# One POOL product of the retention's keys becomes four ACT activations, from the second block on

## The chip, the cores and the metric

The kernel runs on one core of one Trainium2 chip. The metric is the device time of one execution in microseconds (us). Five engines of the core work side by side, each through its own instruction stream: PE (matmul; PEld is its weight load), DVE, ACT, POOL, and SP, which only issues DMAs here.

## The reference

Three layers follow one another on 2304 tokens (4 batches of 576), all in float32:

```python
def _attn_ref(q, k, v):                 # (4, 8, 576, 64)
    scores = scale * np.matmul(q, k.transpose(0, 1, 3, 2))
    gamma = 1.0 - 2.0 ** (-5.0 - np.arange(H))
    Dmat = np.where(rel >= 0, gamma[:, None, None] ** rel, 0.0)
    return np.matmul(scores * Dmat, v)
...
def _moe_ref(x, domain_probs, w1, w2):  # 4 experts, all used by every token
    out += p[:, e:e + 1] * (np.maximum(x @ w1[e], 0.0) @ w2[e])
...
def _moe2_ref(...):                     # 8 experts, one per token by argmax of a gate
    out[mask] = gate_w[mask, None] * eom[mask, e, None] * (np.maximum(x[mask] @ w1[e], 0) @ w2[e])
```

The first layer is retention: attention without softmax, with a decay `gamma[h] ** distance` for each of the 8 heads.

## The kernel before

**Retention in chunks.** Each batch has 9 chunks of 64 positions, so there are 36 steps `s`. Within a chunk, masked scores are multiplied with v. Across chunks a state of k times v is carried and decays by `gamma ** 64` a chunk. For that state each key is first multiplied by `gamma ** (64 - i)`, where `i` is its position in the chunk: this product is `ks`. In the key's layout (partition = two halves of 64 positions, four blocks of 64 columns for four heads each) the factor is one number per partition and block: the table `ktab`, 128 x 4. `ks` is 128 x 256 float32 and isn't needed in the last chunk of a batch.

**A step.** `at_step(s)` issues, in this order, the products of q with the carried state (`at_past`, L273), the scores of the next chunk (`at_scores`, L250, then the mask on DVE, L255), the products of scores with v (`at_b`, L282), the state's new part from `ks[s+1]` (`at_state`, L297), the sum of the state on DVE (`at_sum`, L314), the output `xf` on DVE (L331), its float16 high half on ACT (L333) and its low half on POOL (L335), and last `at_split(s + 2)`, which makes `ks[s+2]` (L229). `ks` has three buffers. Its input is the second half of the tile `vkr`, which SP loads four steps ahead (L221), as soon as the buffer of four steps before is free.

**Blocks.** Four steps make one block of 256 tokens. When a block is complete, `x_mix` forms four differences in place in `xf` on POOL (L343), and, two steps later in the source, `x_keep` splits them into two float16 halves: high halves by two activations (L352, ACT), low halves on POOL (L353). The blocks are stored to DRAM and read back later.

**What runs around it.** The first expert's layers run on the finished blocks between the steps: `l1_first` (L515, with relu and split on ACT L501 and DVE L502) for blocks 0 to 4, and `l2` (L665, L673). After each such unit a hook runs one retention step. Meanwhile the expert weights are combined on POOL (L446) and split into float16 halves on ACT (L200, L201) and DVE (L202). From about 155 us on there is no retention work left, and the rest of the experts, the routing and the second expert layer follow.

**Order.** The kernel's source gives a program order; the compiler's scheduler then sets one fixed order for each engine from dependences, from that program order and from its own estimate of when an input is ready. Each engine works through its list in that order. `tc.issue_after` in the code is a hint to this scheduler, and `pace` holds the instructions that it hangs on.

Of the kernel before, what the change touches and what calls it, by code (L numbers as in the profile page):

```python
# [13 lines left out]
ACTF = mybir.ActivationFunctionType  # L14
ALU = mybir.AluOpType
# [4 lines left out]
B, H, S, D = 4, 8, 576, 64  # L20
# [18 lines left out]
NS = BT // C  # L39
# [91 lines left out]
def kernel(  # L131
# [19 lines left out]
    pe, act, dve, pool, sp = nc.tensor, nc.scalar, nc.vector, nc.gpsimd, nc.sync  # L151
# [17 lines left out]
    def cst(name, *dims):  # L169
        t, at = (ka, of_a) if name in of_a else (kb, of_b)  # L170
        o, n = at[name]
        a = t[:, o:o + n]
        if len(dims) == 2:
            return a.rearrange("p (a b) -> p a b", a=dims[0])
        return a
# [37 lines left out]
    raws, pm, st, uos, pace = {}, {}, {}, {}, {}  # L213
# [10 lines left out]
    def at_split(s):  # L224

        ks = None
        if s % NC < NC - 1:
            ks = at_1.tile([128, 4, D], F32, name="ks")
            pool.tensor_tensor(  # L229
                out=ks, in0=raws[s][1][:, 4:8], in1=cst("ktab", 4, 1).to_broadcast([128, 4, D]), op=ALU.mult  # L230
            )
        raws[s] += (ks,)

    def after(b, a):
# [123 lines left out]
    def at_step(s):  # L358

        at_open(s)  # L360
        at_past(s)
        if s + 1 < NSTEP:
            at_scores(s + 1)
        at_b(s)
        if s + 1 < NSTEP:
            at_state(s + 1, s)
            at_sum(s + 1, s)
        at_out(s)
        if s + 2 < NSTEP:
            at_split(s + 2)  # L370
# [710 lines left out]
    def opening(s):  # L1081
# [3 lines left out]


    at_split(0)
    at_scores(0)
    at_open(-1)
    at_state(0, -1)  # L1090
    at_sum(0, -1)
    at_split(1)
    opening(0)
    opening(1)
# [40 lines left out]
        out=p_sb, in0=p_sb, scalar=SO1, in1=ps_inv.to_broadcast([128, NT, E1]), op0=ALU.mult, op1=ALU.mult  # L1135
# [294 lines left out]
```

## Time and profile before

| | |
|---|---|
| median of 3 runs | 1009.02 us (1006.04 to 1009.07) |
| profiled execution | 1009.17 us, its span 1007.3 us |
| busy in the span | PE 963.7, DVE 578.2, ACT 527.0, POOL 411.8 us |
| retention's steps | from the start to about 160 us |

The span runs from the first to the last instruction of the profiled execution; 1.9 us of its time lie outside. Busy time of an engine is the time in which it executes; a wait is idle time that a profile row puts down to whatever released it. Lines such as L297 are those of the kernel's source, which is printed above.

### The profile page before, as it was taken

What the parts mean: (1) busy time and instruction counts of PE and PEld (TensorE: products, weight loads), DVE (VectorE), ACT (ScalarE), POOL (GpSimd) and SP (SyncE); (2) the same over time, 40 slices, a digit from 0 to 9 for tenths busy, and PEclk for the clock granted to TensorE, in tenths of its full rate; (3) what the DMA queues carried; (4) which work ended last, traced back from release to release, by engine and by line L of the source; (5) the groups of instructions that cost most, each with busy time, mean ns of one, the idle gap of its engine ahead of it and who ended that gap; (6) DMA issues with size and microseconds to landing.
All of it is one profiled execution on the core that took longest, in us unless ns stands there. A gap on an engine that the chain in (4) does not pass through costs nothing. (4 is left out here: it accounts for less than half of the span.)

```text
span 1007.3 us, 31905 instructions
## 1 busy us (share of the span) xinstructions
PE 963.7 (96%) x13507; PEld 827.4 (82%) x13507; DVE 578.2 (57%) x1297; ACT 527.0 (52%) x1001; POOL 411.8 (41%) x432
## 2 busy tenths in 40 slices
PE   5889999999999999999999999999999999999995
PEld 5566677889999999999999999999988677777773
DVE  5645462377767777776777676788888211211210
ACT  3235352487767777767778676666643112212221
POOL 3798874344436324525433453243223212112211
PEclk9999999999999999999999999999999999999998
DMA  9869875247455777556768725778946615554691
GB/s 336 281 225 320 265 238 195 71 153 249 137 177 174 246 272 233 189 183 177 228 205 275 271 85 152 215 201 206 233 133 233 232 43 218 199 231 137 254 395 48
DMA packets 95939, 209.48 MB, mean 208 GB/s; under 512 B 21486, under 2 KB 42222, under 8 KB 93488
## 3 DMA queue, kind: packets, MB, share of 16 engines
q1 hardware_dynamic: 82784, 159.20, 47.7%
q0 software_dynamic: 13008, 48.20, 15.0%
q8 instruction: 108, 1.77, 0.7%
q14 instruction: 39, 0.32, 0.1%
HBM read 197.88 MB, written 52.99 MB: 249 GB/s over the span
## 5 line engine op out<-in xcount | busy, mean ns | idle before, releaser
L628 PEld LDWEIGHTS <-op 128*128 128x128 f16 x2604 | 245.4, 98 | 27.0 <-issue 1.9
L562 POOL TENSOR_TENSOR op<-sm,op 128x512 f16<-128x512 f32 x124 | 142.3, 1157 | 279.8 <-ACT op L561 279.5
L543 PEld LDWEIGHTS <-wm_a 128*128 128x128 f16 x3264 | 192.8, 98 | 7.5 <-issue 3.6
L543 PE MATMUL ph<-xc,wm_a 128*128 128x128 f16 x2112 | 132.2, 219 | 2.9 <-DVE pq L603 2.9
L561 ACT ACTIVATE op<-sm 128x512 f16<-128x512 f32 x124 | 77.4, 633 | 81.5 <-DVE sm L566 81.5
L1048 DVE SCALAR_TENSOR_TENSOR h_s<-p_h,h_s 128x512 f16<-128x512 f32 x40 | 27.6, 691 | 159.1 <-ACT h_s L1047 159.1
L1055 PE MATMUL p_y<-wm_a,h_s 128*128 128x512 f16 x480 | 107.2, 379 | 0.5 <-DVE h_s L1048 0.5
L446 POOL TENSOR_TENSOR wr<-wr 128x512 f32<-128x512 f32 x64 | 81.2, 1274 | 43.1 <-ACT pz L200 39.4
L202 DVE TENSOR_TENSOR s<-pz,s 128x512 f16<-128x512 f32 x128 | 85.4, 683 | 22.4 <-ACT s L201 22.4
L628 PE MATMUL pv<-wm_a,op 128*128 128x256 f16 x792 | 97.6, 273 | 0.0
L628 PE MATMUL px<-wm_a,op 128*128 128x256 f16 x744 | 91.4, 272 | 1.1 <-DVE acc L636 1.1
L1055 PEld LDWEIGHTS <-h_s 128*128 128x128 f16 x480 | 46.7, 98 | 52.4 <-DVE h_s L1048 0.7
L200 ACT ACTIVATE pz<-sr 128x512 f32<-128x512 f32 x128 | 75.4, 603 | 17.0 <-DVE rk L784 10.6
L543 PEld LDWEIGHTS <-wm_b 128*128 128x128 f16 x1296 | 76.9, 98 | 2.2 <-issue 0.9
L1058 POOL DMA_INDIRECT out_dram<-y_s,sidxm x17 | 17.2, 1013 | 146.1 <-ACT y_s L1057 129.0
L201 ACT ACTIVATE s<-pz 128x512 f16<-128x512 f32 x128 | 73.7, 598 | 0.6
L1047 ACT ACTIVATE h_s<-p_h 128x512 f16<-128x512 f32 x40 | 23.9, 597 | 79.1 <-PE p_h L1038 73.2
L636 DVE SCALAR_TENSOR_TENSOR acc<-px,p_sb,acc 128x256 f32<-128x256 f32 x124 | 59.0, 476 | 8.3 <-PE px L628 8.2
L1038 PEld LDWEIGHTS <-wm_b 128*128 128x128 f16 x1056 | 60.0, 98 | 2.8 <-issue 0.6
L1057 ACT ACTIVATE y_s<-p_y,x_g 128x512 f32<-128x512 f32 x20 | 13.7, 687 | 92.5 <-PE p_y L1055 78.9
L1038 PE MATMUL p_h<-x_s,wm_b 128*128 128x128 f16 x1056 | 61.6, 219 | 0.3 <-issue 0.2
L200 ACT ACTIVATE pz<-wr 128x512 f32<-128x512 f32 x100 | 59.6, 607 | 2.3 <-DVE wm_a L202 1.2
(203 smaller groups left out, 1729.7 us busy)
## 6 DMA issues: line engine op xcount, KB each, us to landing
wm_a<-w2d SPq DMA_DIRECT2D x20, 2048.0 KB, 9.0
wr<-in_w_dram SPq DMA_DIRECT2D x40, 512.0 KB, 6.4
wm_b<-w1d SPq DMA_DIRECT2D x10, 2048.0 KB
wm_a<-w1d SPq DMA_DIRECT2D x10, 2048.0 KB
sr<-in_w1s_dram SPq DMA_DIRECT2D x64, 256.0 KB, 4.5
w1d<-s SPq DMA_DIRECT2D x64, 256.0 KB, 6.2
sr<-in_w2s_dram SPq DMA_DIRECT2D x64, 256.0 KB, 4.9
w2d<-s SPq DMA_DIRECT2D x64, 256.0 KB, 4.3
```

What stands on the lines that cost most here:

```text
L200: act.activation(out=z, in_=raw, func=ACTF.Copy, scale=scale)
L201: act.activation(out=hi, in_=z, func=ACTF.Copy)
L202: dve.tensor_tensor(out=lo, in0=z, in1=hi, op=ALU.subtract)
L446: pace["pool"] = pool.tensor_tensor(out=quarter(e, n, k, to), in0=quarter(e, n, k, x), in1=quarter(e, n, k, y), op=op)
L543: pe.matmul(bank[:, i], lhsT=w[:, k, u, 128 * i:128 * i + 128], rhs=x[:, v, d, k], start=(first and i == 0 and n == 0), stop=(n == 5), ski ...
L561: act.activation(out=hi, in_=s, func=ACTF.Copy)
L562: pool.tensor_tensor(out=lo, in0=s, in1=hi, op=ALU.subtract)
L628: pe.matmul(out, lhsT=o[a][:, v, k], rhs=w[c][:, k, u], start=(first and n == 0), stop=(n == 11), skip_group_check=True,)
L636: dve.scalar_tensor_tensor(out=a, in0=src, scalar=p_sb[:, b * TB + i, e:e + 1], in1=a, op0=ALU.mult, op1=ALU.add)
L1038: pe.matmul(ph[:, j], lhsT=w[k][:, x, f * 128:(f + 1) * 128], rhs=xs[:, y, k], start=(n == 0), stop=(n == 3 * KD - 1),)
L1048: dve.scalar_tensor_tensor(out=lo, in0=ph, scalar=0.0, in1=hi, op0=ALU.max, op1=ALU.subtract)
L1055: pe.matmul(po, lhsT=h[:, a, k], rhs=w[k][:, b], start=(n == 0), stop=(n == 3 * KF - 1))
```

## The change

For the first six chunks (`s < NS + 2`, with NS = 4) the keys are multiplied on POOL as before. For all later ones the same product is made by four activations on ACT, one for each block of 64 columns, each with its own scale per partition. Nothing else is edited; `ks` has the same shape, type, buffers and reader.

```diff
         if s % NC < NC - 1:
             ks = at_1.tile([128, 4, D], F32, name="ks")
-            pool.tensor_tensor(
-                out=ks, in0=raws[s][1][:, 4:8], in1=cst("ktab", 4, 1).to_broadcast([128, 4, D]), op=ALU.mult
-            )
+            k = raws[s][1][:, 4:8]
+            if s < NS + 2:
+                pool.tensor_tensor(out=ks, in0=k, in1=cst("ktab", 4, 1).to_broadcast([128, 4, D]), op=ALU.mult)
+            else:
+                for i in range(4):
+                    act.activation(out=ks[:, i], in_=k[:, i], func=ACTF.Copy, scale=cst("ktab")[:, i:i + 1])
```

## Rows read from the trace of the kernel before

**Rows 1.** The page's first part: span and busy time.
```profile
span 1007.3 us, 31905 instructions
...
PE 963.7 (96%) x13507; PEld 827.4 (82%) x13507; DVE 578.2 (57%) x1297; ACT 527.0 (52%) x1001; POOL 411.8 (41%) x432
```

**Rows 2.** Busy time by stretch: length, PE, PEld, DVE, ACT, POOL, clock, DMA.
```profile
25.00:150.00 125.00, 112.62 (x2316) 79.39 (x2314) 70.05 (x203) 51.62 (x105) 103.16 (x130) 0.97 0.80 265
```

**Rows 3.** Waits of PE from 0 to 400 us: total, times, longest.
```profile
PE uo L297 <- POOL ks L229: 6.4, 4, 2.6
```

**Rows 4.** Timeline of PE: start, us, instruction, idle before it and releaser.
```profile
52.53 0.46 PE L297 MATMUL uo<-vkr,ks 64*64 64x64 f32 x16 [1.71 <-POOL ks L229]
...
59.16 0.52 PE L297 MATMUL uo<-vkr,ks 64*64 64x64 f32 x16 [2.61 <-POOL ks L229]
...
63.23 0.46 PE L297 MATMUL uo<-vkr,ks 64*64 64x64 f32 x16
...
126.18 0.46 PE L297 MATMUL uo<-vkr,ks 64*64 64x64 f32 x16 [1.79 <-POOL ks L229]
```

**Rows 5.** Two stretches after those waits, columns as in rows 2.
```profile
59.00:63.00 4.00, 3.84 (x73) 2.85 (x73) 1.52 (x6) 2.90 (x7) 4.00 (x6) 0.57 0.47 187
127.00:131.00 4.00, 4.00 (x30) 2.77 (x32) 0.90 (x4) 0.54 (x2) 3.94 (x7) 0.59 0.82 293
```

**Rows 6.** Timeline of POOL around the waits.
```profile
51.86 0.61 POOL L229 TENSOR_TENSOR ks<-vkr,ka 128x256 f32<-128x256 f32 x1
...
55.68 0.68 POOL L335 TENSOR_TENSOR xc<-xf,xc 128x256 f16<-128x256 f32 x1
...
58.42 0.68 POOL L229 TENSOR_TENSOR ks<-vkr,ka 128x256 f32<-128x256 f32 x1
58.99 0.79 POOL L343 TENSOR_TENSOR xf<-xf 128x256 f32<-128x256 f32 x1
...
125.41 0.71 POOL L229 TENSOR_TENSOR ks<-vkr,ka 128x256 f32<-128x256 f32 x1
```

**Rows 7.** Timeline of SP: the load of chunk 11's `vkr`.
```profile
46.11 0.35 SPq L221 DMA_DIRECT2D vkr<-in_vk_dram  x1
```

**Rows 8.** DMA issues from 40 to 70 us: count, KB each, median us to landing.
```profile
qkr<-in_qk_dram SPq DMA_DIRECT2D x8, 320.0 KB, 5.2
```

**Rows 9.** Line 229 from 25 to 150 us: duration ns min/median/max.
```profile
L229 POOL TENSOR_TENSOR ks<-vkr,ka x26: 610/671/1056, 27.0 to 144.0; 128x256 f32<-128x256 f32 x26
```

**Rows 10.** Groups by form from 0 to 330 us: busy, mean ns, idle before.
```profile
L673 ACT ACTIVATE acc<-po,p_sb 128x512 f32<-128x512 f32 x10 | 6.8, 682 | 7.4 <-PE po L665 7.4
...
L501 ACT ACTIVATE ht<-ph 128x512 f16<-128x512 f32 x16 | 9.5, 595 | 14.3 <-PE ph L515 14.3
...
L191 ACT ACTIVATE wg_sb<-wgr 128x64 f16<-128x64 f32 x1 | 0.2, 248 | 0.0
```

**Rows 11.** Timeline of ACT.
```profile
39.17 1.14 ACT L352 ACTIVATE xc<-xf 128x512 f16<-128x512 f32 x2
...
58.57 0.63 ACT L352 ACTIVATE xc<-xf 128x512 f16<-128x512 f32 x1 [11.51 <-POOL xf L343]
59.11 0.40 ACT L333 ACTIVATE xo<-xf 128x256 f16<-128x256 f32 x1
...
76.93 0.60 ACT L501 ACTIVATE ht<-ph 128x512 f16<-128x512 f32 x1 [0.62 <-PE ph L515]
...
99.89 0.42 ACT L333 ACTIVATE xo<-xf 128x256 f16<-128x256 f32 x1 [1.85 <-DVE xf L331]
...
120.87 0.63 ACT L352 ACTIVATE xm<-xf 128x512 f16<-128x512 f32 x1 [8.06 <-POOL xf L343]
```

**Rows 12.** Timeline of DVE: step 8's `xf`.
```profile
48.12 0.42 DVE L331 TENSOR_TENSOR xf<-uo,ka 128x256 f32<-128x256 f32 x1
```

**Rows 13.** Timeline of PE: a wait for DVE.
```profile
81.02 0.46 PE L273 MATMUL uo<-qkr,sn 64*64 64x64 f32 x16 [0.33 <-DVE xf L331]
```

**Rows 14.** Waits of PE from 150 to 790 us, the longest.
```profile
PE ph L543 <- DVE pq L603: 3.6, 5, 0.8
```

## The prediction

> **What bounds the kernel now.** I read the page first. PE is busy for 963.7 of 1007.3 us [rows 1], so the end moves only if PE's idle time, or the work of a slow-clocked PE, moves. The change touches the retention's stage alone, so I read that stage by itself: from 25 to 150 us PE is busy for 112.62 of 125 us, POOL for 103.16 (83%) and ACT for 51.62 (41%) [rows 2]. POOL is the loaded engine here, and the edit takes work from it and gives it to a half idle one. Whether that is worth anything is read from PE's list of waits: PE waited 6.4 us in four places for POOL's `ks` [rows 3], and the timeline shows the three that matter, 1.71 us in step 9, 2.61 us in step 10 and 1.79 us in step 27 [rows 4] (the fourth is the remaining 0.3).
>
> After the second and third of them the granted clock falls: its mean is 0.57 over 59 to 63 us and 0.59 over 127 to 131 us [rows 5], that is, most of each stretch at 1.2 instead of 2.4 GHz. With PE busy nearly throughout, 4 x (1 - 0.57) = 1.7 us and 4 x (1 - 0.59) = 1.6 us of work were lost. The first wait, of 1.71 us alone, was not followed by such a fall. So POOL's lateness costs 6.4 + 3.3 = 9.7 us, the ceiling of the gain. It would carry through: between 150 and 790 us the longest total that PE waits for one producer is 3.6 us in five pieces [rows 14], for work of its own pace, so no fixed event later on would swallow the lead.
>
> **What the change removes.** 26 of the POOL products, of median 0.671 us [rows 9], 17.4 us off POOL. It is not their sum that counts but their place. POOL's list is fixed and full there: step 10's `ks` runs at 58.42 us, among the four products of `x_mix` (L343) that go before and after it, although its input was asked for at 46.11 [rows 6, 7] and a load of that size lands after 5.2 us [rows 8], thus near 51.3. The same in step 27: `ks` runs at 125.41 [rows 6]. PE, with the product at the head of its list, holds the expert's matmuls behind it. Taken off POOL, `ks` no longer waits for any of this.
>
> **What the change adds.** 4 x 26 = 104 activations of 128x64. The trace has one of that size with a plain number as scale, 248 ns; a scale per partition is seen in L673, 682 ns against 595 ns for L501 of the same size, so 87 ns more; together 335 ns [rows 10]. Alone, four take 1.34 us. Back to back they overlap: two L352 take 1.14 us together where one takes 0.63 [rows 11], 0.12 saved per follower, so four take 1.34 - 3 x 0.12 = 0.98 us. Bounds 0.98 to 1.34 us a chunk; since the four are written in a row and have the same input, I take 1.0. That is 26 us on ACT, which rises from 51.62 to about 78 of 125 us: it has the room.
>
> Does it cost PE anything? Between two units ACT often waits longer than 1 us, for example 1.85 us before 99.89 [rows 11]: there the four are covered. Where the weights are being split too it isn't so: before 76.93 ACT idled for 0.62 us [rows 11], and shortly after, at 81.02, PE already waits 0.33 us for DVE's `xf` [rows 13], which stands behind ACT's results in DVE's list. An extra 1.0 us there becomes about 0.4 to 1.0 us of PE; the weight splits come in this density twice within the retention's stage. So 1 to 2 us if nothing is absorbed, nothing if the scheduler puts the four elsewhere; I take 1.0.
>
> **Where the four land in ACT's list** decides the rest, and the trace of before can't show it. ACT is held for 11.51 us before 58.57 and for 8.06 us before 120.87, each time by an `x_keep` activation (L352) that waits for POOL's `x_mix` [rows 11]. What is behind it waits too: step 8's `xf` was written at 48.12 + 0.42 us [rows 12], and its activation L333 ran only at 59.11 [rows 11]. The Trainium skill, page TensorE: Matmul & The Clock Gate, section Architectural detail, says that ACT's queue is strictly first in, first out; by that rule any `ks` placed behind such an activation is as late as POOL's was, and the row on L333 agrees.
>
> POOL's order tells something of the scheduler's estimates. Step 9's `ks` (51.86) stands ahead of `x_mix`, so its input was held ready before; on ACT it should come ahead of L352. Step 10's stands between `x_mix`'s third and fourth product, the 58.42 row just ahead of the 58.99 row [rows 6]: held ready about when the third ended, which is also what releases the first L352. I take it to come just ahead, since its step is earlier in the source; this is the weak point. Step 11's `ks` came after POOL's whole `x_mix`, so it probably lands behind both L352.
>
> The sum for steps 9 to 11: without the first two waits and the slow clock PE would want step 11's `ks` at 63.23 [rows 4] - 1.71 - 2.61 - 1.0 (the part of the clock's loss before that point) = 57.9 us. One thing is late next on the way: the low half L335 of step 7, which the first unit of block 1 reads, ends on POOL at 55.68 + 0.68 [rows 6], less 0.6 for the product gone ahead of it, 55.8; PE would want it near 55.6, so 0.2 is lost: 58.1. ACT's two L352 follow `x_mix`'s end, 58.99 + 0.79 [rows 6] less two products, 58.5; with one L352, L333 and the other ahead of it, `ks` runs from about 59.4 to 60.4. So PE goes on at 60.5 instead of 63.23: a gain of 2.7 us, and 0.7 us of clock after that point: 3.4. Ends: all freed, 1.71 + 2.61 + 1.7 - 0.2 = 5.8 gained; step 10's `ks` behind both L352 as well, so that PE goes on at about 59.7 instead of 59.16 and the clock falls as before: 0.5 lost.
>
> Step 27: `ks` is behind two L352 at worst, which then run at 120.3 to 121.7 (0.6 earlier, with one product fewer ahead), then two L333 and perhaps one L673; done by 124.0, while PE asks at 124.4 (126.18 - 1.79). So the wait of 1.79 and the 1.6 us of clock go: 3.4 gained. The fourth wait gives 0.3.
>
> Sum: 3.4 + 3.4 + 0.3 - 1.0 = 6.1 us. From the profiled execution's 1009.17 us, which is 0.15 above the median of the runs, that is 1003.1; against the median, 1002.9. Since the ends for steps 9 to 11 reach further down from my value (to a loss of 0.5) than up, I put the number at 1003.5.
>
> **The rivals.** (1) Everything is freed: step 11's `ks` too stands ahead of `x_keep` and the four cost nothing: 9.7 - 0.2 = 9.5 gained, 999.7. For it speaks that ACT is half idle; against it POOL's order at 62 us. (2) The wait moves from POOL to ACT: step 10's `ks` stands behind L352, so POOL still sets it. Then 3.4 + 0.3 - 0.5 - 1.0 = 2.2 gained, 1007.0, within 0.3% of before (3 us is about what a measurement of this kernel can tell from no change). (3) Slower: step 9's `ks` stands behind the L352 that is held until 58.57. L352 would end near 58.5, `ks` near 59.6, so PE goes on at 59.7 in place of 52.53: 7.2 lost; step 10's 2.61 is not paid again, so 4.6. If the same placing holds step 26 behind the L352 of 120.87, another 1.5 to 2 us and a fall of the clock (1.6) are paid there, and step 27's gain only offsets that: with crowding 1.0 the sum is +4 to +5, 1013.5. It decides from the point at which that one `ks` is two places later in the list than I take it. Its place on POOL, one `x_mix` earlier, speaks against it.
>
> **How the numbers follow.** My forecast has 0.42, rival 1 0.18, rival 2 0.22, rival 3 0.18 (some of it, with one trap only and the gain of step 27, ends within 0.3%). Faster by over 0.3%: 0.60. Within 0.3%: rival 2 and a little of 3, 0.25. Slower: 0.15. The range reaches from rival 1's time, 999.5, to between rivals 2 and 3, 1011.0. The likeliest case's own range is 1000.5 to 1006: steps 9 to 11 give between 2 and 5.8, crowding costs 0 to 2.
>
> **What would show it.** Right: PE's waits for `ks` at L297 are gone at step 27 and reduced at steps 9 to 11, with ACT as the releaser of what is left; the clock is 1.00 after 126 us; POOL falls by about 17 us and ACT rises by about 26 from 25 to 150 us; one new activation takes 0.25 to 0.34 us. Wrong: PE waits of over 2 us for ACT's `ks`, behind an L352 that POOL holds; many short PE waits for DVE's `xf`; or a gain at 130 us that is gone by 790.

## The result and the profile after

| | median | runs | profiled execution | its span |
|---|---|---|---|---|
| before | 1008.94 us | 4 | 1009.17 us | 1007.3 us |
| after | 1021.07 us (1019.67 to 1023.15) | 4 | 1019.67 us | 1017.9 us |

The ratio is 1.0132, 95% interval 1.0111 to 1.0153: the change made the kernel slower, by about 12 us by the medians, where 5.5 us of gain were forecast, and the time is outside the range. All lines after the edit move by three: L273 is now L276, L297 is L300, L331 is L334, L352 is L355, L501 is L504. The new activations are L234.

The page's first part after shows that the work went where it was sent: ACT's busy time is up by 22.9 us against [rows 1], POOL's is down by 14.4.

```profile
span 1017.9 us, 31974 instructions
...
PE 966.3 (95%) x13507; PEld 830.1 (82%) x13507; DVE 578.3 (57%) x1297; ACT 549.9 (54%) x1105; POOL 397.4 (39%) x406
```

The instructions of the new line, with the shortest, median and longest duration in ns, and what ACT stood waiting for ahead of them (us in total, times):

```profile
L234 ACT ACTIVATE ks<-vkr,ka x104: 331/334/349, 26.0 to 153.9; 128x64 f32<-128x64 f32 x104
...
its engine sat idle before it (us, times) until:
  DMA vkr<-in_vk_dram: 26.6, 12
```

One activation takes 334 ns, as worked out (335). But the line that matters is the last: twelve times ACT reached a `ks` whose keys had not landed, and stood still for 26.6 us in all. PE's waits from 0 to 400 us show the other end of it:

```profile
PE uo L276 <- DVE xf L334: 12.5, 7, 3.8
...
PE uo L300 <- ACT ks L234: 3.2, 1, 3.2
...
PE po L668 <- issue: 1.1, 1, 1.1
```

The 6.4 us for POOL's `ks` [rows 3] are gone, and one wait of 3.2 us for ACT's has come in their place. New are 12.5 us for `xf`, where before had 0.7. Those waits in the timeline of PE (start, us, instruction, idle before it and its releaser), and at 96.42 the matmuls of an expert's unit whose relu is followed below:

```profile
60.42 1.20 PE L300 MATMUL uo<-vkr,ks 64*64 64x64 f32 x16 [3.18 <-ACT ks L234]
...
84.26 0.46 PE L276 MATMUL uo<-qkr,sn 64*64 64x64 f32 x16 [2.09 <-DVE xf L334]
...
96.42 2.79 PE L518 MATMUL ph<-xc,wm_a 128*128 128x256 f16 x24
...
106.86 0.44 PE L276 MATMUL uo<-qkr,sn 64*64 64x64 f32 x13 [3.83 <-DVE xf L334]
...
141.52 0.71 PE L276 MATMUL uo<-qkr,sn 64*64 64x64 f32 x16 [2.28 <-DVE xf L334]
156.65 0.46 PE L276 MATMUL uo<-qkr,sn 64*64 64x64 f32 x16 [2.20 <-DVE xf L334]
```

The longest one, 3.83 us before 106.86, can be followed back engine by engine. DVE's timeline:

```profile
103.68 0.69 DVE L505 SCALAR_TENSOR_TENSOR ht<-ph,ht 128x512 f16<-128x512 f32 x1 [5.95 <-ACT ht L504]
...
106.29 0.42 DVE L334 TENSOR_TENSOR xf<-uo,ka 128x256 f32<-128x256 f32 x1
```

`xf` was written at 106.29 because DVE stood for 5.95 us in front of L505, which needs the relu L504 from ACT; `xf` is behind it in DVE's list. ACT's timeline just before:

```profile
58.41 1.15 ACT L355 ACTIVATE xc<-xf 128x512 f16<-128x512 f32 x2 [5.07 <-POOL xf L346]
...
60.03 1.05 ACT L234 ACTIVATE ks<-vkr,ka 128x64 f32<-128x64 f32 x4
...
95.03 1.06 ACT L234 ACTIVATE ks<-vkr,ka 128x64 f32<-128x64 f32 x4 [5.32 <-DMA vkr<-in_vk_dram]
...
97.77 1.06 ACT L234 ACTIVATE ks<-vkr,ka 128x64 f32<-128x64 f32 x4 [0.80 <-DMA vkr<-in_vk_dram]
...
100.27 0.83 ACT L234 ACTIVATE ks<-vkr,ka 128x64 f32<-128x64 f32 x3 [1.13 <-DMA vkr<-in_vk_dram]
101.00 0.67 ACT L676 ACTIVATE acc<-po,p_sb 128x512 f32<-128x512 f32 x1
101.57 0.34 ACT L234 ACTIVATE ks<-vkr,ka 128x64 f32<-128x64 f32 x1
101.81 0.40 ACT L336 ACTIVATE xo<-xf 128x256 f16<-128x256 f32 x1
102.34 0.82 ACT L234 ACTIVATE ks<-vkr,ka 128x64 f32<-128x64 f32 x3
103.07 0.57 ACT L504 ACTIVATE ht<-ph 128x512 f16<-128x512 f32 x1
103.55 0.58 ACT L200 ACTIVATE pz<-wr 128x512 f32<-128x512 f32 x1
```

The relu's input was complete at 96.42 + 2.79 = 99.21 us, and it ran at 103.07: 3.86 us late. In front of it in ACT's list stood the `ks` of chunks 20, 21 and 22 (95.03, 97.77 and 100.27), each of which had to wait for its keys, and three quarters of chunk 23's. When the relu's input was complete, ACT still stood until 100.27 for chunk 22's keys; the other 2.8 us are work that had piled up behind these waits: seven activations of `ks`, one of L676 and one of L336. Chunk 22's `ks` was not urgent: PE first reads it in step 21, at 107.89. SP's timeline has the loads of `vkr` and of the expert's weights:

```profile
86.65 0.38 SPq L221 DMA_DIRECT2D vkr<-in_vk_dram  x1
...
88.80 0.82 SPq L221 DMA_DIRECT2D vkr<-in_vk_dram  x1
...
92.36 0.33 SPq L221 DMA_DIRECT2D vkr<-in_vk_dram  x1
...
96.15 0.38 SPq L221 DMA_DIRECT2D vkr<-in_vk_dram  x1
...
104.16 0.33 SPq L413 DMA_DIRECT2D wr<-in_w_dram  x1
104.58 0.38 SPq L221 DMA_DIRECT2D vkr<-in_vk_dram  x1
```

The loads go out in the order of the chunks, and those of 86.65 to 96.15 are chunks 20 to 23 (the twenty-first to the twenty-fourth load from the start). From the issue at 86.65 to the first use at 95.03 it is 8.4 us, from 88.80 to 97.77 9.0, from 92.36 to 100.27 7.9; each of these waits ended with the landing. The loads stand where they stood in the source. Before the change chunk 20's was issued at 82.56 us, in the timeline of SP, and its `ks` followed on POOL:

```profile
82.56 0.37 SPq L221 DMA_DIRECT2D vkr<-in_vk_dram  x1
```

```profile
91.67 0.71 POOL L229 TENSOR_TENSOR ks<-vkr,ka 128x256 f32<-128x256 f32 x1
```

That is 9.1 us after the issue, and POOL didn't wait. ACT came to the same chunk's `ks` at 89.71 (95.03 - 5.32), 3.1 us after its issue. So the keys weren't late for PE; ACT's list came to them too early. After that the wait feeds itself: SP's waits from 25 to 160 us have one of 4.4 us in which a weight load (the one of 104.16) is held by ACT, and the next load of keys is issued behind it. The row names `ks`; what ended on ACT just before 104.16 is L200, a reader of the weights' tile, which stands behind the relu (103.55 + 0.58 = 104.13).

```profile
SPq L413 <- ACT ks L234: 4.4, 1, 4.4
```

Last, the windows (length, busy time of PE, PEld, DVE, ACT and POOL, granted clock, DMA share, GB/s) of the stretches behind three of PE's waits:

```profile
56.00:68.00 12.00, 8.82 (x147) 6.89 (x146) 3.98 (x14) 7.70 (x25) 11.12 (x16) 0.72 0.65 221
...
104.00:116.00 12.00, 8.48 (x170) 7.19 (x171) 7.42 (x23) 6.71 (x20) 6.31 (x8) 0.86 0.73 245
...
138.00:148.00 10.00, 7.72 (x166) 6.41 (x164) 5.62 (x16) 5.98 (x17) 3.88 (x6) 0.83 0.49 167
```

Each lies partly at 1.2 GHz (the first for all of 60 to 66 us); length times (1 - clock) is 3.4 + 1.7 + 1.7 = 6.8 us, against 3.3 behind the two waits of before [rows 5].

**Where the time was lost.** The start of PE's product with `ks` (L297, L300 after) in the same step of both traces gives the lag step by step, and the single matmul that opens block 5 of the first expert (171.01 us before, 181.74 after) ends the stage. Below it is called the marker.

| step | before | after | lag |
|---|---|---|---|
| 9 | 52.53 | 50.30 | -2.23 |
| 10 | 59.16 | 54.57 | -4.59 |
| 11 | 63.23 | 60.42 | -2.81 |
| 12 | 66.12 | 66.20 | +0.08 |
| 17 | 85.32 | 88.56 | +3.24 |
| 20 | 97.41 | 99.89 | +2.48 |
| 21 | 101.27 | 107.89 | +6.62 |
| 22 | 105.60 | 113.74 | +8.14 |
| 26 | 120.65 | 128.73 | +8.08 |
| 27 | 126.18 | 132.28 | +6.10 |
| 28 | 131.66 | 136.10 | +4.44 |
| 29 | 135.47 | 142.82 | +7.35 |
| 33 | 151.09 | 161.39 | +10.30 |
| marker | 171.01 | 181.74 | +10.73 |

The gains of steps 9, 10 and 27 are there. Then 2.9 us go at step 12, 8.0 from step 12 to 26, and 6.3 from step 28 to the marker. The lag of the span is 10.6 us: what is lost here is carried to the end.

The relus show the same without PE. For the 12 units of the first expert whose input was complete between 55 and 158 us, take the time from the end of the unit's last matmul to the start of its relu: the sum is 0.6 us before and 23.2 us after.

### The profile page after: what moved, and what is told of

Read it like the earlier page. It is cut to its first block, busy times and chain, and to the rows that moved or that the text cites. A ratio compares the mean times of both kernels' runs of the same rounds, so it can differ in the third digit from the quotient of the medians.

```text
span 1017.9 us, 31974 instructions
## 1 busy us (share of the span) xinstructions
PE 966.3 (95%) x13507; PEld 830.1 (82%) x13507; DVE 578.3 (57%) x1297; ACT 549.9 (54%) x1105; POOL 397.4 (39%) x406
## 5 line engine op out<-in xcount | busy, mean ns | idle before, releaser
L200 ACT ACTIVATE pz<-sr 128x512 f32<-128x512 f32 x128 | 75.6, 603 | 17.9 <-DVE rk L787 10.7
L200 ACT ACTIVATE pz<-wr 128x512 f32<-128x512 f32 x100 | 59.4, 605 | 2.1 <-DVE wm_c L202 0.9
```

Source lines behind the costliest of these rows:

```text
L200: act.activation(out=z, in_=raw, func=ACTF.Copy, scale=scale)
```

## The experiments

The first theory after the result: ACT's wait for the keys costs the time, since the scheduler placed `ks` before the relu. Rivals: the work of the 104 activations itself (crowding); the hold behind `x_keep`; the lateness of the loads as such. Medians and ratios are against runs of the kernel before on the same chip, 15 to 24 in each batch with medians of 1008.6 to 1009.5 us (after: the 4 above). Marker, waits and clock are from one profiled execution each. Single runs of the kernel before spread over 7 us, so verdicts rest on the ratios and the marker serves to find the place.

| | marker | median, ratio (95%) | PE's wait for `xf` in front of L273, for `ks` | clock loss | ACT's wait for keys |
|---|---|---|---|---|---|
| before | 171.01 | 1008.94 | 0.7, 6.4 | 3.4 | none |
| after | 181.74 | 1021.07, 1.0132 (1.0111 to 1.0153) | 12.5, 3.2 | 6.8 | 26.6 |
| e1_work_no_wait | 169.07 | 1018.05, 1.0075 (1.0048 to 1.0102), not comparable | 3.8, 0.5 | 1.7 | 0 |
| e2_wait_no_work | 176.21 | 1018.23, 1.0094 (1.0060 to 1.0128) | 7.2, 7.7 | 0 | 30.6 |
| e3_behind_output | 175.25 | 1013.70, 1.0045 (1.0025 to 1.0064) | 6.2, 4.0 | 3.4 | 10.2 |
| e4_keys_before_keep | 170.86 | 1009.56, 1.0005 (0.9989 to 1.0020) | 6.1, 0.2 | 1.7 | 6.4 |
| e5_loads_earlier | 179.28 | 1015.37, 1.0060 (1.0040 to 1.0080) | 11.8, 0 | 3.5 | 25.0 |
| e6_keep_and_loads | 169.50 | 1007.71, 0.9995 (0.9980 to 1.0010) | 5.6, 0 | 0 | 0 |
| e7_pool_order | 174.31 | 1011.91, 1.0028 (1.0009 to 1.0047) | 4.1, 4.6 | 3.4 | none |
| e8_four_chunks_on_act | 175.83 | 1013.46, 1.0062 (1.0033 to 1.0091) | 3.3, 3.7 | 6.7 | 9.8 |
| e9_one_activation | 173.13 | one run, total not comparable | 6.9, 1.9 | 1.7 | 0 |
| e10_relu_first | 166.57 | 1003.99, 0.9938 (0.9915 to 0.9962) | 2.2, 0.7 | 0 | 0 |
| e11_relu_first_old_loads | 164.34 | 1004.49, 0.9949 (0.9931 to 0.9966) | 2.9, 0 | 0 | 4.7 |
| e12_relu_first_only | 170.45 | 1009.48, 0.9997 (0.9976 to 1.0018) | 3.0, 3.3 | 3.4 | 16.7 |

All in us; the waits for `ks` are those from 25 us on, since the first six chunks are made on POOL in every version; clock loss is the sum of length times (1 - clock) over windows of 12 us from 50 to 158 us.

### The work without the wait, the wait without the work

**e1_work_no_wait.** The four activations read a table that is resident from the start, so they have no keys to wait for.

```diff
-                    act.activation(out=ks[:, i], in_=k[:, i], func=ACTF.Copy, scale=cst("ktab")[:, i:i + 1])
+                    act.activation(out=ks[:, i], in_=x[:, i], func=ACTF.Copy, scale=cst("ktab")[:, i:i + 1])
```

with `x = cst("mask", 4, D)`.

> The four activations per chunk stay on ACT with the same shapes, but read a resident table of constants (the mask) in place of the loaded keys, so that ks holds other values and the retention's result is not the reference's; ACT's work is the same and its wait for the load of vkr is gone. Theory H (head of line: in the changed kernel ACT's list reaches ks before its keys have landed, 26.6 us of waits for that load from 25 to 165 us, which hold the relu L504 and through DVE's list PE): PE's wait for DVE's xf falls from 12.5 to under 3 us, and the time to 1009 us or less. Theory W (it is the work: 26 x 1.06 = 27.6 us more on ACT make its results late): the time stays at 1017 to 1021 us with PE's wait for xf above 8 us. Theory K (the x_keep activations that wait for POOL hold ks): PE's wait for ACT's ks grows, the time stays over 1015 us.

With the same 104 activations the marker is 1.9 us ahead of before, not 10.7 behind. With other numbers in the state the second expert layer's tokens fall to other experts, PE runs 13631 matmuls instead of 13507, and the part behind the marker took 848.2 us instead of 836.3, so only the marker is read; the time of 1009 us that theory H named could not be tested. ACT's work as such isn't the loss of 10.7 us. But ACT's list changed as well. Its timeline shows the four behind the relu (L505) and the splits of the weights, in the time before the next output:

```profile
95.62 0.60 ACT L505 ACTIVATE ht<-ph 128x512 f16<-128x512 f32 x1 [1.05 <-PE ph L519]
96.12 0.60 ACT L200 ACTIVATE pz<-wr 128x512 f32<-128x512 f32 x1
96.75 0.60 ACT L201 ACTIVATE wm_a<-pz 128x512 f16<-128x512 f32 x1
97.24 1.05 ACT L235 ACTIVATE ks<-ka 128x64 f32<-128x64 f32 x4
```

So the run shows that the work in that place doesn't make the loss, but not that it is free: POOL's waits (6.4 us) are gone, and yet the marker is only 1.9 us ahead. The lateness of the relus in sum is 9.4 us, 8.6 of it in the first two units, where `ks` stands in front of them once more, behind `x_keep`; of PE's 3.8 us of waits for `xf` 3.1 come there. That is more than the 3 us theory H allowed. What the work costs in front of the relu, without a wait, is left to e4, e6 and e10.

**e2_wait_no_work.** POOL keeps the product as before; ACT only copies one column of the keys, so it must wait for them but does next to nothing.

```diff
             pool.tensor_tensor(out=ks, ...)
+            if s >= NS + 2:
+                see = at_1.tile([128, 1], F32, name="see")
+                act.activation(out=see, in_=raws[s][1][:, 4, 0:1], func=ACTF.Copy)
```

> POOL makes ks as in the kernel before; in addition, from chunk 6 on, one activation of 128x1 on ACT copies one element of the same keys into a tile that nobody reads. That gives ACT the wait for the load without the work (26 x about 0.2 us). Theory H: ACT waits 10 to 27 us for vkr, PE waits 5 to 12 us for DVE's xf on top of the 6.4 us for POOL's ks, time 1015 to 1025 us. Theory W: as before the change, 1009 us, within 3 us. Theory K: as before the change too.

The copies take 0.20 us each, and the kernel is slower by 0.94%, with an interval that lies clear of no change. Up to 160 us the lists of ACT, DVE and POOL are those of before, operation by operation, but for the added copies. At the marker its profiled execution, the fastest of its runs, is 5.2 us late. The row of ACT's waits from 25 to 165 us is the first below, and its timeline at the place of the longest wait of after follows:

```profile
ACT see L234 <- DMA vkr<-in_vk_dram: 30.6, 16, 7.6
```

```profile
96.88 0.20 ACT L234 ACTIVATE see<-vkr 128x1 f32<-128x1 f32 x1 [3.92 <-DMA vkr<-in_vk_dram]
...
101.53 0.20 ACT L234 ACTIVATE see<-vkr 128x1 f32<-128x1 f32 x1 [0.97 <-DMA vkr<-in_vk_dram]
101.64 0.58 ACT L504 ACTIVATE ht<-ph 128x512 f16<-128x512 f32 x1
```

So the wait alone costs time, by the same way: the relus were late by 13.8 us in sum, and PE waited 7.2 us for `xf`. It still paid POOL's waits too (7.7 us for `ks`), so it isn't after's loss without its gains one for one.

### The order of ACT's list

**e3_behind_output.** A hint to the scheduler: `ks` behind the float16 copy of the output (L336) of the step before.

```diff
-        act.activation(out=hi, in_=xf, func=ACTF.Copy)
+        last_hi.append(act.activation(out=hi, in_=xf, func=ACTF.Copy))
...
+                with tc.issue_after(last_hi[-2].ins):
                     for i in range(4):
                         act.activation(out=ks[:, i], ...)
```

> The changed kernel with one hint more: the four activations for chunk s + 2 come in ACT's list behind the high half of the output of step s - 1 (L333 of before), so about a step later than the scheduler put them. Theory H: the keys have mostly landed by then; ACT's waits for vkr fall from 26.6 to under 8 us, PE's wait for xf from 12.5 to under 4 us; the time is 1001 to 1010 us, with what x_keep's hold costs at step 10 or 11 still in it. Theory W: no change, 1018 to 1022 us. Theory K: the activations stand later, more of them behind x_keep: 1020 us or more.

ACT's wait for keys fell to 10.2 us and the ratio from 1.0132 to 1.0045, both less far than theory H had it. What is left begins with one wait of PE of 3.98 us for ACT's `ks` before 58.19 us, followed by a slow clock: there `ks` stands behind `x_keep`, which POOL holds.

**e4_keys_before_keep.** e3, and `x_keep`'s activations are put behind the last `ks`.

```diff
-        with tc.issue_after(pace["act"].ins):
+        with tc.issue_after((last_ks[0] if last_ks else pace["act"]).ins):
```

> As the kernel with the activations behind the output of step s - 1, and in addition x_keep's activations come behind the last ks activations issued before them, so that no ks of steps 9 to 12 stands behind an activation that waits for POOL. Theory H with K as a second, smaller part: 2 to 4 us less than without this second hint, 998 to 1006 us, no wait of PE for ACT's ks over 1 us. Theory W: 1018 to 1022 us. H without K: the same time as without the second hint.

That wait is gone (0.2 us for `ks` in all), the ratio falls from 1.0045 to 1.0005, with intervals that don't meet. So the hold behind `x_keep` that the prediction had in mind is real, and a smaller part: 1013.70 - 1009.56 = 4.1 us. The time stays above the 998 to 1006 us that were expected: 6.1 us of waits for `xf` are left, of 1.4 us at most each.

**e5_loads_earlier.** After, with five buffers for `vkr` and its load issued one step earlier.

```diff
+        t = at_raw.tile([128, 10, D], F32, name="vkr", bufs=5)
...
+        if s + 4 < NSTEP:
+            vks[s + 4] = v_load(s + 4)
```

> The changed kernel, with its activations where the scheduler puts them, but the keys' tile vkr has five buffers and is loaded one step earlier in the source. Nothing else differs. Theory H (ACT's list waits for the load): ACT's waits for vkr fall from 26.6 to under 10 us, PE's wait for xf from 12.5 to under 5 us, the marker (the one 128x512 product py<-wm_a that opens block 5, at 171.0 us before the change and 181.7 after it) comes at 170 to 176 us. If the scheduler uses the earlier load to put the activations earlier too, the waits stay and so does the time: then H is neither shown nor refuted. Theory W (the work itself): marker at 180 us or later.

ACT still waited 25.0 us: with earlier loads the scheduler moved `ks` forward in ACT's list as well. The run therefore says little about lateness as such; the ratio of 1.0060 lies below after's, but its order is another one.

**e6_keep_and_loads.** e4 and e5 together.

> Keys before keep (activations behind the output of step s - 1, x_keep behind the activations) and the earlier load together. There ACT still waited 6.4 us for vkr and PE 6.1 us for xf. If those two belong together, both fall below 3 us, the marker comes at 166 to 169 us and the time is 1003 to 1007 us. If PE's wait for xf comes from ACT's and DVE's lists being full (crowding), it stays at 5 to 6 us and the marker at 170 to 171 us.

Now ACT waits for no keys at all, and the kernel is as fast as before, 0.9995, no more. 5.6 us of waits for `xf` are still there. The next run's rows say why. In e6, ACT's list has the four in front of the relu, so the relu is late by their work (13.6 us in sum over the 12 units, `xf`'s own delay included):

```profile
99.16 1.05 ACT L247 ACTIVATE ks<-vkr,ka 128x64 f32<-128x64 f32 x4
100.11 0.57 ACT L517 ACTIVATE ht<-ph 128x512 f16<-128x512 f32 x1
```

**e10_relu_first.** e6, and `ks` also behind the relu of the unit just issued (`pace["act"]`).

```diff
-                with tc.issue_after(last_hi[-2].ins):
+                with tc.issue_after(last_hi[-2].ins), tc.issue_after(pace["act"].ins):
```

> The same with four activations, and they come in ACT's list also behind the relu of the unit that ran before their step, so that a relu whose input is ready no longer waits 0.8 us for them. If the rest of the loss is this place (head of line in small), PE's wait for xf falls from 5.6 to under 2 us, the marker comes at 164 to 167 us, and the time is 1002 to 1005 us, faster than before the change by 0.3 to 0.7%. If it is crowding that no order mends, the marker stays at 169 to 170 us and the time at 1007 to 1009 us.

ACT's timeline at the same unit has the two the other way round:

```profile
98.90 0.58 ACT L517 ACTIVATE ht<-ph 128x512 f16<-128x512 f32 x1
99.38 1.05 ACT L247 ACTIVATE ks<-vkr,ka 128x64 f32<-128x64 f32 x4
```

PE's waits for `xf` fall from 5.6 to 2.2 us, and the ratio to 0.9938: this version is faster than before, with an interval that doesn't meet e6's. Against e6 it gains 3.7 us by the medians, and 5.8 by the ratios, which set each against before on its own chip. The relus' lateness falls from 13.6 to 3.6 us. Since neither of the two waits for keys, this is the price of the work in front of the relu, as near as a hint can show it: the scheduler moved some of DVE's list, and ACT's weight splits near 26 us, with it.

**e11_relu_first_old_loads.** e4 with the same hint, so the loads stay where they were. ACT's and DVE's lists are those of e10, operation by operation; on POOL three weight products come earlier.

> The same order of ACT as with the relu first, operation by operation in the stage, but vkr is loaded with four buffers and at the old place. This pair differs by the load alone. Theory H: ACT's waits for vkr come back in part, 3 to 8 us, the marker is 1 to 4 us later than with the earlier load. If nothing waits for the late loads any more (what stands behind them isn't urgent), the two are within 1 us.

ACT waited 4.7 us for keys, in four pieces, and the time is that of e10: 0.9949 against 0.9938, intervals overlapping. Against e4, from which its source differs by the hint alone, it gained 1009.56 - 1004.49 = 5.1 us by the medians, 5.7 by the ratios. Late keys cost nothing that can be measured here, once no urgent operation stands behind them.

**e12_relu_first_only.** After with the one hint `tc.issue_after(pace["act"].ins)` and nothing else.

> The changed kernel with one hint: the four activations come behind the relu of the unit before their step; x_keep and the loads stay as in the changed kernel. Theory H: the loss of 10.7 us at the marker was mostly the relu standing behind activations that wait for a load, so the marker comes at 170 to 176 us, with up to 4 us of waits of PE for ACT's ks behind x_keep left over; time 1007 to 1014 us. If the place of the activations ahead of the relu doesn't matter: 180 us and 1019 us.

This is the sharpest of the runs: the same work, loads at the same place in the source, and ACT still waits 16.7 us for keys, but each `ks` behind the relu of the unit before it. ACT's timeline:

```profile
96.04 1.07 ACT L235 ACTIVATE ks<-vkr,ka 128x64 f32<-128x64 f32 x4 [2.71 <-DMA vkr<-in_vk_dram]
...
98.19 0.58 ACT L505 ACTIVATE ht<-ph 128x512 f16<-128x512 f32 x1
98.67 1.06 ACT L235 ACTIVATE ks<-vkr,ka 128x64 f32<-128x64 f32 x4
```

The wait before 96.04, and the work piled up behind it, still hold one relu, that of 98.19, by 2.3 us. Over the 12 units the relus' lateness is 3.9 us instead of 23.2, and the ratio goes from 1.0132 to 0.9997. What keeps it from e11's time stands in PE's timeline, the wait behind `x_keep` in step 11:

```profile
59.74 1.20 PE L301 MATMUL uo<-vkr,ks 64*64 64x64 f32 x16 [3.32 <-ACT ks L235]
```

The lag against before, from PE's product with `ks` as in the table above, for the runs that tell this apart:

| step | after | e2 | e4 | e12 | e11 |
|---|---|---|---|---|---|
| 10 | -4.59 | +0.78 | -3.65 | -5.43 | -1.68 |
| 12 | +0.08 | +0.78 | -4.72 | -0.59 | -3.31 |
| 17 | +3.24 | +2.41 | -2.99 | -0.19 | -3.24 |
| 22 | +8.14 | +5.44 | 0.00 | +2.51 | -4.32 |
| 28 | +4.44 | +2.49 | -2.09 | -1.18 | -6.90 |
| 33 | +10.30 | +4.79 | +0.67 | +0.28 | -5.84 |

After and e12 lose the same lead, 4.7 and 4.8 us, between steps 10 and 12 (behind `x_keep`). From there to step 22 after loses 8.1 us; e2, with the wait but no work, 4.7; e4, with the work in front of the relu and few waits, 4.7; e12 3.1, of which 2.2 are one wait of PE before 108.11 with no releaser shown; e11 gains 1.0. A hint doesn't move one operation alone: against after, e12 has some outputs, weight splits and sums of the state in other places of ACT's and DVE's lists too.

### Other ways

**e7_pool_order.** No activation at all; POOL's list is reordered instead, `x_mix` one step later, and `x_mix` and the mixing of weights behind the last `ks`.

```diff
-        at_done(s - 1, x_mix)
         at_step(s)
+        at_done(s - 2, x_mix)
...
+            with tc.issue_after(last_ks[0].ins):
                 pool.tensor_tensor(out=m[:, ox, oy], ...)
```

> POOL makes ks as in the kernel before, nothing on ACT; only POOL's order is set: x_mix is issued a step later in the source, and x_mix and the combinations of the weights come behind the last ks issued before them. If what hurt the kernel before was only the place of three products in POOL's list, the 6.4 us of waits for ks fall below 2 us, the slow clock after them goes, and the marker comes at 163 to 167 us, the time at 1000 to 1005 us. If POOL is simply too full (83% busy from 25 to 150 us), waits of 4 us or more appear elsewhere and the marker stays at 169 to 173 us.

PE still waited 4.6 us for POOL's `ks`, and 4.1 for `xf`; the ratio is 1.0028, and the marker, 174.31, is later than either guess. This reordering of POOL's list doesn't give the gain.

**e8_four_chunks_on_act.** Only the chunks whose `ks` was late on POOL, and the one after (10, 11, 12 and 28), go to ACT, with `x_keep` behind them.

```diff
-            if s < NS + 2:
+            if s not in (10, 11, 12, 28):
```

> Only chunks 10, 11, 12 and 28, three of which PE waited for in the kernel before and one beside them, are multiplied on ACT, with x_keep behind them; all others stay on POOL. ACT then waits for a load only where little stands behind it. Theory H: the gain without the loss; PE's waits for ks under 1.5 us in sum, for xf under 2 us, marker at 162 to 166 us, time 999 to 1005 us. Theory W or crowding: the same here, so this run tells only whether the gain foreseen was there at all. If new waits of 3 us or more arise from the other order, marker at 168 us or later.

New waits came in other places: 3.75 us for POOL's `ks` before 65.03 us, 2.37 us without a shown releaser before 97.18, and a clock loss of 6.7 us. The ratio is 1.0062, far from the gain expected. A change of a few chunks gives a new list everywhere, and the old waits don't tell where the new ones are.

**e9_one_activation.** e6 with one activation of 128x256 for all four blocks, with the first block's scale.

```diff
-                    for i in range(4):
-                        last_ks[:] = [act.activation(out=ks[:, i], in_=k[:, i], ..., scale=cst("ktab")[:, i:i + 1])]
+                    last_ks[:] = [act.activation(out=ks, in_=k, ..., scale=cst("ktab")[:, 0:1])]
```

> The kernel with keys before keep and the earlier load, but one activation of 128x256 with the first head's factors in place of four of 128x64, so that three of four heads decay wrongly; it is read by the marker (the 128x512 product that opens block 5, 169.5 us with four), not by its end, since the routing sees other values. One activation takes about 0.5 us where four take 1.05. If PE's remaining 5.6 us of waits for DVE's xf come from the length of the work that stands ahead of the relu, they fall to 1 to 3 us and the marker to 165 to 168 us. If they come from something else in ACT's or DVE's list, they stay and the marker is at 169 to 170 us.

Meant to measure the work of the four, it changed the order too: PE waited 1.94 us for ACT's `ks` before 65.26, where e6 has no wait, and 1.94 for POOL's before 17.66, where e6 has 0.7. The marker came 3.6 us later with less work on ACT. It settles nothing on the price of the work.

## Why the prediction failed

**Right: what bounded the kernel, and what the change frees.** POOL's three waits at steps 9, 10 and 27 are gone. Steps 27 and 28 gave 8.08 - 4.44 = 3.6 us, forecast 3.4. At step 10 the kernel was 4.59 us ahead.

**Right: the price of the operations.** One activation 334 ns (335), four together 1.05 to 1.06 us (1.0). Right as well: step 11's `ks` stands behind both activations of `x_keep`, and PE goes on at 60.42 us (60.5). That it fits to 0.1 us is luck: the four began at 60.03 instead of 59.4, since one of L676 came between, and PE began when the first of them was done, not the fourth. The lag at the marker is carried to the end (10.7 and 10.6 us).

**Mis-sized: steps 9 to 11.** They were to give 3.4 us and gave nothing by step 12 (+0.08). The sum left a wait of 60.5 - 58.1 = 2.4 us at step 11 and yet counted 0.7 us of clock as won after it. The wait was 3.18 us, and over 56 to 68 us the clock lost 3.4 us. A wait of 2.61 us was followed by such a fall in the very trace that was read [rows 4, 5]; the chance of the same was to be charged to the wait that the sum itself left behind.

**Failed: "Does it cost PE anything?"** This is the step that turned the sign. It put the price at 1.0 us, at most 2, as a matter of ACT's room for 1.0 us of work in a unit, and "nothing if the scheduler puts the four elsewhere". From step 12 to 26 the cost was 8.0 us, from step 28 to the marker 6.3: 14.3 us. It isn't the work as such: e1 has all of it, mostly behind the relu, and is ahead of before. It is the place in ACT's list, in front of the relu, together with keys that had not landed. The prediction took it that a `ks` off POOL runs when its keys are there, and looked for a hold on ACT only behind `x_keep`. The scheduler's order put up to three chunks' `ks` ahead of the unit's relu, before their keys had landed; ACT stood, the relu was late (3.86 us at the worst wait), DVE's `xf` behind it too, and PE waited 12.5 us and then ran partly at 1.2 GHz. That the wait does this is shown by e2, which has it without the work, and by e12, which has the same work and 16.7 us of the waits, behind a relu. The second part of the price is work: the four in front of the relu cost 3.7 to 5.8 us where ACT waits for no keys (e10 against e6), and about as much where it waits 4.7 to 6.4 us (e11 against e4). So crowding, taken as 1.0, was mis-sized as well. Behind the relu it is less by these 4 to 6 us; that it is nothing there isn't shown.

Of the prediction's signs of being wrong, the waits for `xf` came: seven, of up to 3.83 us. Its one slower rival (3, to 1013.5 us) didn't: step 9's `ks` ran on ACT at 49.74, ahead of `x_keep` at 58.41. The loss took a way that none of its rivals had.

The Trainium skill, page TensorE: Matmul & The Clock Gate, section Architectural detail, calls ACT's queue strictly first in, first out. The row of 103.07 agrees: a relu with its input complete at 99.21 stood behind activations that waited for a load. The prediction used that rule for one operation in front, and not for its own four.

**The sum.** Forecast -3.4 - 3.4 - 0.3 + 1.0 = -6.1; measured to the marker +0.1 (steps to 12) + 8.0 - 3.6 + 6.3 = +10.8, the lag of 10.7 but for rounding.

**Was there a clue?** Not in POOL's waits. In the trace of before, POOL stood 12.6 us, in seven pieces, waiting for `vkr` in front of `ks`, but 10.9 of them, in five pieces, lie between 7 and 21 us, in chunks that POOL keeps. For the chunks that move, from 25 to 165 us, it was this:

```profile
POOL ks L229 <- DMA vkr<-in_vk_dram: 1.6, 2, 0.9
```

POOL came to them late, 9.1 us after the issue for chunk 20, and ACT early, 3.1 us after it. The prediction read from one load near 46 us that keys land in 5.2 us [rows 7, 8], and did not ask when ACT's list would come to them, nor how long a load takes at 90 us (7.9 to 9.0 us to the first use, above).

**The gain was there to be had.** With three hints on the order (e11) the time is 1004.49, and with earlier loads besides (e10) 1003.99, near the forecast of 1003.5. Both are faster than either kernel. That doesn't confirm the forecast, which had neither the hints nor the cost that they take away.

**Open.** Which of the scheduler's estimates put `ks` ahead of the relu stands in no trace; that it judged the keys to land earlier than they do is argued only. How after's loss splits between ACT's wait, the work behind it and the clock isn't settled: e2 lost 5.2 us at the marker of its profiled execution, with the clock undisturbed, and 9 by the median. The runs with hints compare whole orders of the lists, not one swap; only e2 leaves the lists of before as they were. PE's waits of 1 to 2.4 us that no recorded event ended (1.1 us after, 2.2 in e12, 2.4 in e8) are unexplained.

## What to carry to other kernels

Before moving an operation to a half idle engine, ask what will stand behind it in that engine's list and when its input really lands in that stretch; an engine that works in order gives its idle time only to operations that are ready. Pin the moved operation behind the urgent one: here one hint took away a loss of 12 us, and three turned it into a gain of 5. A wait that a sum leaves in place is to be charged the chance of a slow clock as well.

## What the runs showed of the hardware

The clock's fall isn't told by the length of PE's wait alone. In after the clock was 1.00 in the windows behind the waits of 2.09 us (84 to 90 us) and 2.20 us (156 to 168), and 0.83 behind one of 2.28. In e2 a wait of 2.60 us at the place where before had 2.61 was followed by 1.00 from 58 to 70 us; before had 0.57 over 59 to 63 [rows 5]. e2's window:

```profile
58.00:70.00 12.00, 8.46 (x196) 6.97 (x196) 4.83 (x18) 5.24 (x14) 11.92 (x18) 1.00 0.73 251
```

The wait came in step 10, in front of the product with `ks`, in both; what differed isn't known. So the clock's share of a forecast of this size, 1.7 us behind most of these waits and 3.4 behind the one of 3.18, is a chance and not a certainty.
